# One DMA transpose in place of a plain load and TensorE transposes for the second 256 tokens of x's first two slabs, W1's second block on another queue, and a later transpose of the small vectors

## The chip, the cores and the metric

The kernel runs on one core of a Trainium2 chip. The metric is the device time of one execution, in microseconds (us); lower is better. Times of the kernel as it was come from three runs and from one execution that was taken with a hardware profiler.

## The reference

The input x has 2048 tokens of 640 features. Two results are computed from it and mixed by a gate per token.

```python
g = _sigmoid((x * gate_w).sum(-1, keepdims=True))
a = _A_ref(x, Lambda_re, Lambda_im, B_re, B_im, C_re, C_im, log_dt, Dskip)
b = _B_ref(x, w1, b1, w2, b2)
return g * a + (1 - g) * b
```

Here `_A_ref` is a state space layer: x is projected to 640 complex states (`B_bar`), a linear recurrence runs over the 2048 tokens, `h = Lam_bar * h + Bu[t]`, and the states are projected back, `2 * Re(h @ C^T) + x * Dskip`. `_B_ref` is a dense layer with 1728 hidden features, `gelu(x @ w1 + b1) @ w2 + b2`. The change concerns only how the first tokens of x and of W1 reach the first matmuls, `x @ w1`.

## The kernel before

**Tiles.** The tokens are cut into four quarters q of 512. Matmuls contract over partitions, so x is needed transposed: `xT[q]` has 128 partitions (features within a slab) by five slabs k of 128 features by 512 tokens. A "slab" of x is one k. Where x is loaded by a DMA transpose (`load_T`, L336 to L342, called by `xtrans`, L353), it lands in `xT` directly. `xn` holds x untransposed, tokens on partitions; the gates and the last stage use it.

**The first stage.** `m1_first` (L643 to L664) computes the first eight blocks of 128 hidden features (index jf) for the first quarter. All eight PSUM banks accumulate at once; the loop over slabs k is the outer one, so that work can begin when the first slab of x and the first block of W1's rows (`w1load(0, ...)`, 128 rows by 1024 columns, 256 KB) are there. For slab 0 the first six jf are done in two halves of 256 tokens each (`steps`, L648); everything else is done with 512 tokens. `w1load(k, ...)` brings W1's rows for slab k; `w1_r0` and `w1_r1` (L379) bring the other columns. After the first stage, `m1(0, NW)` (L668) goes on with the remaining jf in banks that the gelu instructions of ScalarE (L662) have freed, then `bproj(0)` projects to the states, and so on.

**How slabs 0 and 1 of x arrive.** A DMA transpose at the very start would be one way. The kernel before instead loads the first two slabs (256 features) untransposed, in two loads of 256 tokens, `xna0` and `xna1` (L369 to L371, into `xn[0]`), and TensorE transposes them against an identity (L421 to L431): `xt0` and `xt1` for the first 256 tokens of slabs 0 and 1, `xt2` and `xt3` for the second. VectorE copies each pair from PSUM to `xT` (`xc0` to `xc3`, L434). Slabs 2, 3 and 4 come by DMA transposes (L374, L376). Before that TensorE runs six matmuls on constants (`f_warm`, L413) and one more behind the first transposes (`f_fill`, L438).

**The small vectors.** Lambda, log_dt and b1 are loaded as rows of a 128 by 128 tile `rows` (L390 to L394), which GpSimd has zeroed first (`rz`, L386). One TensorE transpose, `cols` (L455), turns them into columns; VectorE copies them (L460). From there a chain of short instructions runs: exp on ScalarE (L465), angles on VectorE (L470, L485 to L493), exp and sine on ScalarE (L478, L498, L499), then the first gelu (L662). ScalarE loads an activation table ahead of exp, of sine and of gelu.

**What sets the order of work.** Nothing is ordered by hand. Every piece of work is an `op` with an engine, a modelled duration, reads and writes (from which its dependencies follow), and a priority (`Prog.op`, L157). `Sched.order` (L43 to L83) runs a list schedule on modelled times: it takes the engine that can act earliest (ties by name), and on it, among the pieces whose dependencies are done by then in the model, the one with the lowest priority number.

```python
                d_e = max(t_eng[e], min(r for _, r in released[e]))
...
            avail = [(it.prio, it.idx, it) for it, r in released[e] if r <= now + 1e-9]
            avail.sort(key=lambda x: (x[0], x[1]))
            it = avail[0][2]
```

The result is one fixed order per engine. The engines that issue DMAs here are SyncE ("sp", queue q1 in the profile), ScalarE ("act", queue q10) and GpSimd ("pool", queue q0). At the start SyncE issues, in this order: `xna0`, `xna1`, W1's second block (k=1, L372), its third block (L373), the transpose of slab 2 (L374), W1's fourth block (L375), the transpose of slabs 3 and 4 (L376), W1's fifth block (L377), the rest of W1 (L379), then the transposes of B. ScalarE issues W1's first block (L389; it reads "rz", so it is modelled to wait for GpSimd's memset, 0.2 us), then the six loads into `rows`. Matmuls get rising priorities 1, 2, 3, ... (`pe_prio`, L612); `cols` has 20.5.

**Later use of xn.** The other three slabs of the first quarter, untransposed, are loaded much later, by `xnb` (L594), for the gates.

Of the kernel before, what the change touches and what calls it, by code (L numbers as in the profile page):

```python
# [9 lines left out]
BF16 = mybir.dt.bfloat16  # L10
# [137 lines left out]
class Prog:  # L148
# [8 lines left out]
    def op(self, name, eng, dur, reads, writes, fn, prio=None, lat=0.0, after=()):  # L157
        deps = {}
        for k in reads:
            for w in self.last_w.get(k, ()):  # L160
                deps[w.idx] = w
        for k in writes:
            for w in self.last_w.get(k, ()):
                deps[w.idx] = w
            for r in self.last_r.get(k, ()):
                deps[r.idx] = r
        for a in after:
            deps[a.idx] = a
        deps = list(deps.values())
        E = self.E  # L170

        def run(eg, deps=deps, eng=eng, fn=fn):
            E.wait(eng, *[d.done for d in deps if not (eng == "pe" and d.eng == "pe")])
            return fn()

        it = self.sch.add(name, eng, dur, deps, run, prio=prio, lat=lat)
        for k in writes:
            self.last_w[k] = [it]
            self.last_r[k] = []
        for k in reads:  # L180
            self.last_r.setdefault(k, []).append(it)
        return it


def bass_gated_mix__ssm_conv_s5__dense_activation_gelu__prompt_kernel(
# [18 lines left out]
    _, S, D = A_x.shape  # L204
# [3 lines left out]
    KD = D // 128  # L208
# [13 lines left out]
    x2 = A_x[0]  # L222
# [3 lines left out]
    with ExitStack() as es:  # L226

        def SB(name, shape, dt):
            return es.enter_context(nc.sbuf_tensor(name, list(shape), dt))

        xT = [SB(f"xT_{i}", [128, KD, 512], BF16) for i in range(NQ)]
        xn = [SB(f"xn_{i}", [128, 4, D], BF16) for i in range(2)]
# [10 lines left out]
        cols = SB("cols", [128, 3 * KP + NF], FP32)  # L243
# [10 lines left out]
        ident = SB("ident", [128, 128], BF16)  # L254
# [34 lines left out]
        late = [w1f[:, i * D:(i + 1) * D] for i in range(2 * NE + 2 + NO)]  # L289
# [4 lines left out]
        PS = [es.enter_context(nc.psum_tensor(f"ps{i}", [128, 512], FP32)) for i in range(8)]  # L294
# [13 lines left out]
        op = pr.op  # L308

        def inc(eng, ins):  # L310
            return E.inc(eng, ins, eng + "_s")

        def dma_inc(eng, ins, sem):
            SEM(sem)
            E.count.setdefault(sem, 0)
            ins.then_inc(sems[sem], 16)
            E.count[sem] += 16
            return (sem, E.count[sem])

        def d_act(n):  # L320
            return 0.26 + n * 0.00084
# [4 lines left out]
        def d_mm(n):  # L326
            return n / 2400.0 + 0.004


        def load(name, eng, sem, dst, src, writes, prio, dur=0.5, lat=2.5, reads=(), after=()):  # L330
            def fn():
                with nc.allow_non_contiguous_dma(reason="columns of small vectors"):
                    return dma_inc(eng, engines[eng].dma_start(dst, src), sem)
            return op(name, eng, dur, reads, writes, fn, prio=prio, lat=lat, after=after)

        def load_T(name, sem, pairs, writes, prio, dur, lat=3.0, reads=()):  # L336
            def fn():
                t = None
                for dst, src in pairs:
                    t = dma_inc("sp", nc.sync.dma_start_transpose(dst, src), sem)  # L340
                return t
            return op(name, "sp", dur, reads, writes, fn, prio=prio, lat=lat)  # L342
# [6 lines left out]
        NW = 8  # L349
# [9 lines left out]
        def w1load(k, eng, prio, reads=()):  # L359
            edges = [0] + ([WSPLIT[k] * 128] if k in WSPLIT else []) + [FW]  # L360
            for i, (f0, f1) in enumerate(zip(edges, edges[1:])):
                load(f"w1_{k}{i}", eng, f"l_w1{k}{i}", W1sb[:, k, f0:f1], B_w1[k * 128:(k + 1) * 128, f0:f1], [("w1", k, i)], prio=prio + 0.1 * i, lat=2.6, reads=reads)

        def w1tok(k, jf):
            return ("w1", k, int(jf >= WSPLIT.get(k, NW)))

        KN = 2

        for h in range(2):  # L369
            load(f"xna{h}", "sp", f"l_xna{h}", xn[0][:, 2 * h:2 * h + 2, 0:KN * 128],  # L370
                 x2[h * 256:(h + 1) * 256, 0:KN * 128].rearrange("(c p) d -> p c d", p=128), [("xna", h)], 0.2 * h, dur=0.45, lat=2.0 + 0.4 * h)  # L371
        w1load(1, "sp", 1)  # L372
        w1load(2, "sp", 4)  # L373
        xtrans(0, range(2, 3), 5, 1.15)  # L374
        w1load(3, "sp", 6)  # L375
# [6 lines left out]
        ROWS = {"lre": (0, A_Lambda_re), "lim": (KP, A_Lambda_im), "ldt": (2 * KP, A_log_dt), "b1a": (3 * KP, B_b1[0:nmain])}  # L382
# [4 lines left out]

        op("rz", "pool", 0.2, (), list(ROWS) + [("b1b", 0), ("b1b", 1), "rz"], f_rz, prio=-90)
        w1load(0, "act", -110, reads=["rz"])  # L389
        for i, (nm, (r0, src)) in enumerate(ROWS.items()):  # L390
            src = src.rearrange("(k p) -> k p", p=128)
            load(nm, "act", "l_" + nm, rows[r0:r0 + src.shape[0], :], src, [nm], prio=-100 + i, dur=0.4)
# [25 lines left out]

        op("warm", "pe", 2.7, (), [("bank", 4)], f_warm, prio=-1000)

        for i, (k, c0, c1) in enumerate(((0, 0, 2), (1, 0, 2), (0, 2, 4), (1, 2, 4))):  # L421
            bank = (7, 6, 7, 6)[i]
            pt = PS[bank][:, :].bitcast(BF16)[:, 0:(c1 - c0) * 128]

            def f_xt(k=k, pt=pt, c0=c0, c1=c1):
                t = None
                for c in range(c0, c1):
                    t = nc.tensor.transpose(pt[:, (c - c0) * 128:(c - c0 + 1) * 128], xn[0][:, c, k * 128:(k + 1) * 128], ident[:, :])  # L428
                return inc("pe", t)

            op(f"xt{i}", "pe", 0.11 * (c1 - c0), [("xna", c0 // 2), "ident"], [("bank", bank)], f_xt, prio=-990 + i if i < 2 else 3.1 + 0.1 * i)  # L431

            def f_xc(k=k, pt=pt, c0=c0, c1=c1):
                return inc("dve", nc.vector.tensor_copy(out=xT[0][:, k, c0 * 128:c1 * 128], in_=pt))  # L434

            op(f"xc{i}", "dve", 0.42, [("bank", bank)], [("xT", 0, k, c0)], f_xc, prio=-2000 + i)

        def f_fill():  # L438
            t = None
# [1 line left out]
                t = nc.tensor.matmul(PS[3][:, 0:256], one.broadcast_to([128, 128]), one.broadcast_to([128, 256]), start=True, stop=True)  # L441
            return inc("pe", t)

        op("fill", "pe", 0.11, [("xna", 0), "ident"], [("bank", 3)], f_fill, prio=-900)

        XK0 = [[("xT", 0, k)] for k in range(KD)]
        XK0[0] = [("xT", 0, 0, 0), ("xT", 0, 0, 2)]
# [6 lines left out]
        def f_cols():  # L454
            return inc("pe", nc.tensor.transpose(psC, rows[:, :], ident[:, :]))  # L455

        op("cols", "pe", 0.3, list(ROWS) + [("b1b", 0), ("b1b", 1), "ident"], [("bank", 7)], f_cols, prio=20.5)

        def f_cols1():
            return inc("dve", nc.vector.tensor_copy(out=cols[:, :], in_=psC[:, 0:RT + 1]))  # L460
# [128 lines left out]
        for ci, src in enumerate((A_B_re, A_B_im)):  # L589
            for i, (p0, p1) in enumerate(((0, 512), (512, KP * 128))):  # L590
                load_T(f"B{ci}{i}", f"l_B{ci}{i}", [(BT[:, ci, :, p0:p1], src[p0:p1, :])], [("BT", ci, i)], prio=30 + ci + 0.1 * i, dur=0.8 * (p1 - p0) / 128)
        xtrans(1, range(KD), 32, 3.4)
        load("gwb", "sp", "l_gwb", gwb[:, :], gate_w.partition_broadcast(128), ["gwb"], prio=32.2)
        load("xnb", "sp", "l_xnb", xn[0][:, :, KN * 128:D], x2[0:512, KN * 128:D].rearrange("(c p) d -> p c d", p=128),  # L594
             [("xn", 0, 0), ("xn", 0, 1)], 32.4, dur=1.0, lat=6.0, reads=[("xna", 0), ("xna", 1)])
        big = load("w2a", "sp", "l_w2a", W2sb[:, 0:NF - 1, :], B_w2[0:nmain, :].rearrange("(j p) d -> p j d", p=128), ["w2a"], prio=33, lat=8.0)
        load("w2b", "sp", "l_w2b", W2sb[0:FL, NF - 1, :], B_w2[nmain:F, :], ["w2b"], prio=34, lat=4.0)
        load("w2c", "sp", "l_w2c", W2sb[64:64 + FL, NF - 1, :], B_w2[nmain:F, :], ["w2c"], prio=34.2, lat=4.0)
# [13 lines left out]
        def pe_prio():  # L612
            ctr["pe"] += 1
            return ctr["pe"]
# [26 lines left out]


        def m1_first():  # L643
            late = [(0, NW - 1), (1, NW - 1)]
            seq = [(k, jf) for k in range(KD) for jf in range(NW) if (k, jf) not in late]
            i = seq.index((2, NW - 1))
            seq[i:i] = late
            steps = [(0, jf, h) for h in range(2) for jf in range(6)] + [(k, jf, None) for k, jf in seq if k or jf > 5]  # L648
            for k, jf, h in steps:
                t0, t1 = (0, 512) if h is None else (256 * h, 256 * h + 256)  # L650

                def f_mm(jf=jf, k=k, t0=t0, t1=t1):
                    return inc("pe", nc.tensor.matmul(PS[jf][:, t0:t1], W1sb[:, k, jf * 128:(jf + 1) * 128], xT[0][:, k, t0:t1],  # L653
                                                      start=(k == 0 and t0 == 0), stop=(k == KD - 1), skip_group_check=jf < 6))

                op(f"m1_0_{jf}_{k}_{t0}", "pe", d_mm(t1 - t0), (XK0[k] if h is None else XK0[k][h:h + 1]) + [w1tok(k, jf)], [("bank", jf)],
                   f_mm, prio=pe_prio())
            for jf in range(NW):
                ctr["bank"] += 1

                def f_ge(jf=jf):
                    return inc("act", nc.scalar.activation(Gl[0][:, jf, :], PS[jf][:, :], ACT.Gelu_apprx_tanh, bias=b1col[:, jf:jf + 1]))  # L662

                op(f"ge_0_{jf}", "act", d_act(512), [("bank", jf), "b1col"], [("gl", 0, jf)], f_ge, prio=10)  # L664
# [344 lines left out]
        def outsT(q, mid=None):  # L1009
# [104 lines left out]
            op(f"sto{q}", "sp", 0.5, [("xn", q % 2, 0), ("xn", q % 2, 1)], [], f_st, prio=403 + q, lat=3.0)  # L1114

        m1_first()
        m1(0, NW)
        bproj(0)
# [83 lines left out]
```

## Time and profile before

| | us |
|---|---|
| median of 3 runs (lowest, highest) | 212.66 (212.58, 212.69) |
| the profiled execution's own time | 211.84 |
| its span in the trace | 210.5 |
| TensorE busy in the span | 206.9 (98%) |
| VectorE busy | 191.0 (91%) |
| ScalarE busy | 102.7 (49%) |
| DMA engines' mean share, 2 to 3 us / 5 to 6 us | 0.98 / 1.32 |

The span is the time from the first to the last instruction of the profiled execution; about 1.3 us lie around it. Starts in the timeline are us from the span's start. "PE" is TensorE's matmuls, "PEld" its weight loads, "DVE" VectorE, "ACT" ScalarE, "SPq" and "ACTq" the instructions by which SyncE and ScalarE issue DMAs. A line such as L653 is a line of the kernel. Matmuls are pipelined and their ends are modelled: a busy TensorE may still be short of its peak, and the distance from one start to the next says more than a duration. Where many DMAs overlap, the DMA share can come out above 1.

### The profile page before, as it was taken

What the parts mean: (1) busy time and instruction counts of PE and PEld (TensorE: products, weight loads), DVE (VectorE), ACT (ScalarE), POOL (GpSimd) and SP (SyncE); (2) the same over time, 40 slices, a digit from 0 to 9 for tenths busy, and PEclk for the clock granted to TensorE, in tenths of its full rate; (3) what the DMA queues carried; (4) which work ended last, traced back from release to release, by engine and by line L of the source; (5) the groups of instructions that cost most, each with busy time, mean ns of one, the idle gap of its engine ahead of it and who ended that gap; (6) DMA issues with size and microseconds to landing.
All of it is one profiled execution on the core that took longest, in us unless ns stands there. A gap on an engine that the chain in (4) does not pass through costs nothing.

```text
span 210.5 us, 2557 instructions
## 1 busy us (share of the span) xinstructions
PE 206.9 (98%) x987; PEld 95.1 (45%) x1004; DVE 191.0 (91%) x244; ACT 102.7 (49%) x166; POOL 4.2 (2%) x12
## 2 busy tenths in 40 slices
PE   8999999999999999999999999999999999999996
PEld 4544444444444444444444444444444444444444
DVE  2499999999999999999999999899999999899482
ACT  2398556679850533556683222455664253204321
POOL 1000000030000000000000000000010000000000
DMA  6999999999500020053373000006631000006623
GB/s 191 271 230 124 200 204 226 361 190 207 129 0 4 0 50 0 0 107 65 80 61 113 3 0 0 0 2 140 142 87 58 0 0 4 0 2 145 135 71 100
DMA packets 50248, 19.47 MB, mean 93 GB/s; under 512 B 43068, under 2 KB 48828, under 8 KB 50236
## 3 DMA queue, kind: packets, MB, share of 16 engines
q1 hardware_dynamic: 47904, 17.59, 38.2%
q0 software_dynamic: 1600, 1.32, 4.3%
q10 hardware_dynamic: 732, 0.40, 0.7%
q8 instruction: 8, 0.13, 0.3%
q14 instruction: 4, 0.03, 0.1%
HBM read 8.68 MB, written 2.63 MB: 54 GB/s over the span
## 4 chain that ended last, share of the span: by engine, by line
PE 98%; issue 0%; DVE 0%
PE ps L675 22%; PE ps L718 20%; PE ps L1015 20%; PE ps L1085 15%; PE ps L809 5%; PE ps L653 4%; PE ps L922 4%; PE ps L829 1%; PE ps L416 1%; PE ps L696 1%; PE ps L882 1%; PE ps L1050 1%; PE ps L428 0%; PE ps L846 0%; DVE W1sb L954 0%
## 5 line engine op out<-in xcount | busy, mean ns | idle before, releaser
L675 PE MATMUL ps<-xT,W1sb 128*128 128x512 bf16 x214 | 47.5, 379 | 0.3
L762 DVE TENSOR_TENSOR_SCAN W<-atab,V 128x1280 bf16<-128x1280 f32 x16 | 44.3, 2812 | 0.3
L718 PE MATMUL ps<-xT,BT 128*128 128x512 bf16 x196 | 43.3, 379 | 0.2
L1015 PE MATMUL ps<-Gl,W2sb 128*128 128x512 bf16 x192 | 42.8, 379 | 0.2
L682 ACT ACTIVATE Gl<-ps,cols 128x512 bf16<-128x512 f32 x44 | 29.8, 695 | 15.5 <-PE ps L675 15.5
L675 PEld LDWEIGHTS ps<-xT,W1sb 128*128 128x128 bf16 x220 | 21.5, 98 | 26.0
L1085 PE MATMUL ps<-Hb,CT 128*128 128x512 bf16 x150 | 32.9, 379 | 0.0
L729 ACT ACTIVATE U<-ps 128x512 bf16<-128x512 f32 x40 | 23.7, 596 | 15.5 <-PE ps L718 15.5
L718 PEld LDWEIGHTS ps<-xT,BT 128*128 128x128 bf16 x200 | 19.4, 98 | 23.8 <-ACT Gt L704 0.4
L1015 PEld LDWEIGHTS ps<-Gl,W2sb 128*128 128x128 bf16 x195 | 18.9, 98 | 23.3 <-issue 0.7
L1023 ACT ACTIVATE E1T<-ps,cols 128x512 bf16<-128x512 f32 x15 | 10.0, 686 | 26.2 <-PE ps L1015 14.7
L1085 PEld LDWEIGHTS ps<-Hb,CT 128*128 128x128 bf16 x150 | 14.7, 98 | 17.7
L1093 ACT ACTIVATE E2T<-ps 128x512 bf16<-128x512 f32 x15 | 9.0, 597 | 21.7 <-PE ps L1085 21.7
L627 DVE SCALAR_TENSOR_TENSOR trf<-xn,gwb 128x640 bf16<-128x640 bf16 x16 | 13.2, 823 | 0.4
L505 DVE TENSOR_TENSOR V<-V,W 128x1280 bf16<-128x1280 bf16 x16 | 12.5, 821 | 0.3
L505 DVE TENSOR_TENSOR Hb<-Hb,V 128x1280 bf16<-128x1280 bf16 x16 | 12.5, 821 | 0.3
L505 DVE TENSOR_TENSOR V<-mr,U 128x2560 bf16<-128x2560 bf16 x8 | 11.9, 1492 | 0.3
L505 DVE TENSOR_TENSOR Hb<-c,W 128x2560 bf16<-128x2560 bf16 x8 | 11.9, 1490 | 0.2
L809 PE MATMUL ps<-W2sb,Gl 128*128 128x512 bf16 x51 | 11.8, 379 | 0.1
L505 DVE TENSOR_TENSOR V<-s,W 128x2560 bf16<-128x2560 bf16 x8 | 11.9, 1484 | 0.0
L505 DVE TENSOR_TENSOR W<-mi,U 128x2560 bf16<-128x2560 bf16 x8 | 11.9, 1483 | 0.0
L1073 ACT ACTIVATE xT<-xT,cols 128x512 bf16<-128x512 bf16 x15 | 10.0, 712 | 0.0
(103 smaller groups left out, 148.2 us busy)
## 6 DMA issues: line engine op xcount, KB each, us to landing
W2sb<-in_B_w_dram SPq DMA_DIRECT2D x1, 2080.0 KB, 8.4
out_dram<-xn SPq DMA_DIRECT2D x3, 640.0 KB, 5.5
xn<-in_A_x_dram POOLq DMA_DIRECT2D x2, 640.0 KB, 7.0
W1sb<-in_B_w_dram SPq DMA_DIRECT2D x4, 256.0 KB, 4.0
trf<-grow SPq DMA_DIRECT2D x4, 256.0 KB, 4.9
xn<-in_A_x_dram SPq DMA_DIRECT2D x1, 640.0 KB, 7.2
W1sb<-in_B_w_dram SPq DMA_DIRECT2D x1, 480.0 KB, 5.6
W1sb<-in_B_w_dram SPq DMA_DIRECT2D x1, 400.0 KB, 6.4
```

Of the source, the lines that this page charges most:

```text
L505: return inc("dve", nc.vector.tensor_tensor(out=o, in0=a, in1=b, op=o_))
L627: t = inc("dve", nc.vector.scalar_tensor_tensor(out=scr[:, :], in0=xn[q % 2][:, c, :], scalar=1.0, in1=gwb[:, :], op0=ALU.mult, op1=ALU.mu ...
L675: t = nc.tensor.matmul(PS[bank][:, :], W1sb[:, k, jf * 128:(jf + 1) * 128], xT[q][:, k, :], start=(k == 0), stop=(k == KD - 1))
L682: return inc("act", nc.scalar.activation(Gl[q % 2][:, jf, :], PS[bank][:, :], ACT.Gelu_apprx_tanh, bias=b1col[:, jf:jf + 1]))
L718: t = nc.tensor.matmul(PS[bank][:, :], BT[:, ci, kd, k * 128:(k + 1) * 128], xT[q][:, kd, :], start=(kd == 0), stop=(kd == KD - 1))
L729: return inc("act", nc.scalar.activation(dst, src, ACT.Copy, scale=1.0 if ci == 0 else -1.0))
L762: t = inc("dve", nc.vector.tensor_tensor_scan(out=g[:, ci, :], data0=a, data1=v[:, ci, :], initial=0.0, op0=ALU.mult, op1=ALU.add))
L809: t = nc.tensor.matmul(PS[bank][:, :], Gl[q % 2][:, jf, t4 * 128:(t4 + 1) * 128], W2sb[:, jf, 0:DN], start=False, stop=False, skip_group_c ...
L1015: t = nc.tensor.matmul(PS[bank][:, :], W2sb[:, jf, d * 128:(d + 1) * 128], Gl[q % 2][:, jf, :], start=(jf == 0 and not lead), stop=(jf == ...
L1023: return inc("act", nc.scalar.activation(E1T[:, d, :], PS[bank][:, :], ACT.Identity, bias=cols2[:, 0, d:d + 1]))
L1073: return inc("act", nc.scalar.activation(xT[q][:, d, :], xT[q][:, d, :], ACT.Copy, scale=cols2[:, 1, d:d + 1]))
L1085: t = nc.tensor.matmul(PS[bank][:, :].rearrange("p (s t) -> p s t", s=2), CT[:, ci, k, d * 128:(d + 1) * 128], Hb[:, 2 * (q % 2):2 * (q % ...
```

## The change

The second 256 tokens of slabs 0 and 1 no longer come by `xna1`, four TensorE transposes and two VectorE copies. One DMA transpose on SyncE's queue, `xTa`, writes them into `xT[0]`. The first 256 tokens come as before (the load is now called `xna`). W1's second block moves from SyncE's queue to ScalarE's, with priority -109 and no reads. `cols` moves from priority 20.5 to 23.5. In `m1_first`, seven jf instead of six are done in halves for slab 0. Later, `xnb` becomes two loads, one of three slabs for the first 256 tokens and one of all five slabs for the second 256 tokens.

```diff
--- before.py
+++ after.py
@@ -366,10 +366,8 @@
 
         KN = 2
 
-        for h in range(2):
-            load(f"xna{h}", "sp", f"l_xna{h}", xn[0][:, 2 * h:2 * h + 2, 0:KN * 128],
-                 x2[h * 256:(h + 1) * 256, 0:KN * 128].rearrange("(c p) d -> p c d", p=128), [("xna", h)], 0.2 * h, dur=0.45, lat=2.0 + 0.4 * h)
-        w1load(1, "sp", 1)
+        load("xna", "sp", "l_xna", xn[0][:, 0:2, 0:KN * 128], x2[0:256, 0:KN * 128].rearrange("(c p) d -> p c d", p=128), ["xna"], 0, dur=0.45, lat=2.0)
+        load_T("xTa", "l_xTa", [(xT[0][:, 0:KN, 256:512], x2[256:512, 0:KN * 128])], [("xT", 0, k, 2) for k in range(KN)], 0.2, 1.2, lat=2.0)
         w1load(2, "sp", 4)
         xtrans(0, range(2, 3), 5, 1.15)
         w1load(3, "sp", 6)
@@ -387,6 +385,7 @@
 
         op("rz", "pool", 0.2, (), list(ROWS) + [("b1b", 0), ("b1b", 1), "rz"], f_rz, prio=-90)
         w1load(0, "act", -110, reads=["rz"])
+        w1load(1, "act", -109)
         for i, (nm, (r0, src)) in enumerate(ROWS.items()):
             src = src.rearrange("(k p) -> k p", p=128)
             load(nm, "act", "l_" + nm, rows[r0:r0 + src.shape[0], :], src, [nm], prio=-100 + i, dur=0.4)
@@ -418,22 +417,22 @@
 
         op("warm", "pe", 2.7, (), [("bank", 4)], f_warm, prio=-1000)
 
-        for i, (k, c0, c1) in enumerate(((0, 0, 2), (1, 0, 2), (0, 2, 4), (1, 2, 4))):
-            bank = (7, 6, 7, 6)[i]
-            pt = PS[bank][:, :].bitcast(BF16)[:, 0:(c1 - c0) * 128]
-
-            def f_xt(k=k, pt=pt, c0=c0, c1=c1):
+        for k in range(KN):
+            bank = 7 - k
+            pt = PS[bank][:, :].bitcast(BF16)[:, 0:256]
+
+            def f_xt(k=k, pt=pt):
                 t = None
-                for c in range(c0, c1):
-                    t = nc.tensor.transpose(pt[:, (c - c0) * 128:(c - c0 + 1) * 128], xn[0][:, c, k * 128:(k + 1) * 128], ident[:, :])
+                for c in range(2):
+                    t = nc.tensor.transpose(pt[:, c * 128:(c + 1) * 128], xn[0][:, c, k * 128:(k + 1) * 128], ident[:, :])
                 return inc("pe", t)
 
-            op(f"xt{i}", "pe", 0.11 * (c1 - c0), [("xna", c0 // 2), "ident"], [("bank", bank)], f_xt, prio=-990 + i if i < 2 else 3.1 + 0.1 * i)
-
-            def f_xc(k=k, pt=pt, c0=c0, c1=c1):
-                return inc("dve", nc.vector.tensor_copy(out=xT[0][:, k, c0 * 128:c1 * 128], in_=pt))
-
-            op(f"xc{i}", "dve", 0.42, [("bank", bank)], [("xT", 0, k, c0)], f_xc, prio=-2000 + i)
+            op(f"xt{k}", "pe", 0.22, ["xna", "ident"], [("bank", bank)], f_xt, prio=-990 + k)
+
+            def f_xc(k=k, pt=pt):
+                return inc("dve", nc.vector.tensor_copy(out=xT[0][:, k, 0:256], in_=pt))
+
+            op(f"xc{k}", "dve", 0.42, [("bank", bank)], [("xT", 0, k, 0)], f_xc, prio=-2000 + k)
 
         def f_fill():
             t = None
@@ -441,7 +440,7 @@
                 t = nc.tensor.matmul(PS[3][:, 0:256], one.broadcast_to([128, 128]), one.broadcast_to([128, 256]), start=True, stop=True)
             return inc("pe", t)
 
-        op("fill", "pe", 0.11, [("xna", 0), "ident"], [("bank", 3)], f_fill, prio=-900)
+        op("fill", "pe", 0.11, ["xna", "ident"], [("bank", 3)], f_fill, prio=-900)
 
         XK0 = [[("xT", 0, k)] for k in range(KD)]
         XK0[0] = [("xT", 0, 0, 0), ("xT", 0, 0, 2)]
@@ -454,7 +453,7 @@
         def f_cols():
             return inc("pe", nc.tensor.transpose(psC, rows[:, :], ident[:, :]))
 
-        op("cols", "pe", 0.3, list(ROWS) + [("b1b", 0), ("b1b", 1), "ident"], [("bank", 7)], f_cols, prio=20.5)
+        op("cols", "pe", 0.3, list(ROWS) + [("b1b", 0), ("b1b", 1), "ident"], [("bank", 7)], f_cols, prio=23.5)
 
         def f_cols1():
             return inc("dve", nc.vector.tensor_copy(out=cols[:, :], in_=psC[:, 0:RT + 1]))
@@ -591,8 +590,10 @@
                 load_T(f"B{ci}{i}", f"l_B{ci}{i}", [(BT[:, ci, :, p0:p1], src[p0:p1, :])], [("BT", ci, i)], prio=30 + ci + 0.1 * i, dur=0.8 * (p1 - p0) / 128)
         xtrans(1, range(KD), 32, 3.4)
         load("gwb", "sp", "l_gwb", gwb[:, :], gate_w.partition_broadcast(128), ["gwb"], prio=32.2)
-        load("xnb", "sp", "l_xnb", xn[0][:, :, KN * 128:D], x2[0:512, KN * 128:D].rearrange("(c p) d -> p c d", p=128),
-             [("xn", 0, 0), ("xn", 0, 1)], 32.4, dur=1.0, lat=6.0, reads=[("xna", 0), ("xna", 1)])
+        for h in range(2):
+            f0 = KN * 128 * (1 - h)
+            load(f"xnb{h}", "sp", f"l_xnb{h}", xn[0][:, 2 * h:2 * h + 2, f0:D], x2[h * 256:(h + 1) * 256, f0:D].rearrange("(c p) d -> p c d", p=128),
+                 [("xn", 0, h)], 32.4 + 0.1 * h, dur=0.6, lat=6.0, reads=["xna"])
         big = load("w2a", "sp", "l_w2a", W2sb[:, 0:NF - 1, :], B_w2[0:nmain, :].rearrange("(j p) d -> p j d", p=128), ["w2a"], prio=33, lat=8.0)
         load("w2b", "sp", "l_w2b", W2sb[0:FL, NF - 1, :], B_w2[nmain:F, :], ["w2b"], prio=34, lat=4.0)
         load("w2c", "sp", "l_w2c", W2sb[64:64 + FL, NF - 1, :], B_w2[nmain:F, :], ["w2c"], prio=34.2, lat=4.0)
@@ -641,17 +642,16 @@
 
 
         def m1_first():
-            late = [(0, NW - 1), (1, NW - 1)]
-            seq = [(k, jf) for k in range(KD) for jf in range(NW) if (k, jf) not in late]
+            seq = [(k, jf) for k in range(1, KD) for jf in range(NW) if (k, jf) != (1, NW - 1)]
             i = seq.index((2, NW - 1))
-            seq[i:i] = late
-            steps = [(0, jf, h) for h in range(2) for jf in range(6)] + [(k, jf, None) for k, jf in seq if k or jf > 5]
+            seq[i:i] = [(0, NW - 1), (1, NW - 1)]
+            steps = [(0, jf, h) for h in range(2) for jf in range(NW - 1)] + [(k, jf, None) for k, jf in seq]
             for k, jf, h in steps:
                 t0, t1 = (0, 512) if h is None else (256 * h, 256 * h + 256)
 
                 def f_mm(jf=jf, k=k, t0=t0, t1=t1):
                     return inc("pe", nc.tensor.matmul(PS[jf][:, t0:t1], W1sb[:, k, jf * 128:(jf + 1) * 128], xT[0][:, k, t0:t1],
-                                                      start=(k == 0 and t0 == 0), stop=(k == KD - 1), skip_group_check=jf < 6))
+                                                      start=(k == 0 and t0 == 0), stop=(k == KD - 1), skip_group_check=jf < NW - 1))
 
                 op(f"m1_0_{jf}_{k}_{t0}", "pe", d_mm(t1 - t0), (XK0[k] if h is None else XK0[k][h:h + 1]) + [w1tok(k, jf)], [("bank", jf)],
                    f_mm, prio=pe_prio())
```

## The prediction

> **What bounds the kernel now.** I read the page first: busy shares and the chain that ended last.
>
> ```profile
> PE 206.9 (98%) x987; PEld 95.1 (45%) x1004; DVE 191.0 (91%) x244; ACT 102.7 (49%) x166; POOL 4.2 (2%) x12
> ...
> PE 98%; issue 0%; DVE 0%
> ```
>
> TensorE carries the end: nothing but matmuls stands in the chain. So a change counts only as far as it removes matmul time, or moves the moment from which TensorE never waits again. To find that moment I read the timeline of the first 14 us (start, duration, what, and in brackets the idle time before it).
>
> ```profile
> 0.74 0.97 SPq L333 DMA_DIRECT2D xn<-in_A_x_dram  x2
> ...
> 0.97 0.40 ACTq L333 DMA_DIRECT2D W1sb<-in_B_w_dram  x1
> ...
> 2.74 1.20 SPq L340 DMA_TRANSPOSE xT<-in_A_x_dram  x1
> 3.06 0.49 PEld L428 LDWEIGHTS ps<-ident,xn 128*128 128x128 bf16 x4 [0.47 <-DMA xn<-in_A_x_dram]
> ...
> 3.98 0.34 PEld L653 LDWEIGHTS ps<-xT,W1sb 128*128 128x128 bf16 x3 [0.33 <-DVE xT L434]
> ...
> 4.55 0.39 PE L428 MATMUL ps<-ident,xn 128*128 128x128 bf16 x4
> ...
> 5.21 2.06 PEld L653 LDWEIGHTS ps<-xT,W1sb 128*128 128x128 bf16 x14 [0.23 <-DVE xT L434]
> ...
> 7.60 0.22 PE L455 MATMUL ps<-ident,rows 128*128 128x128 bf16 x1
> ...
> 12.06 2.42 ACT L662 ACTIVATE Gl<-ps,cols 128x512 bf16<-128x512 f32 x4
> ```
>
> Three waits: for x (to 3.06), for the first copy (to 3.98), for the copy of the second 256 tokens (to 5.21). After 5.21 the matmuls run back to back into the second stage: each 512-column matmul starts 0.216 us after the last, each 256-column one 0.109. The first matmul with W1's second block (k=1) starts at 6.09. I call that moment K; everything behind it follows at a fixed distance, so the change is worth what it does to K, plus any new wait behind it.
>
> Then I asked for the DMA issues in narrow windows (KB, us from issue to landing). The first four rows are the first x load, W1's first block, the first DMA transpose of x, and a transpose of the same size at 204 us, when the DMA engines are nearly idle; the last two are the queues between 2.65 and 3.0 us (packets, MB, share).
>
> ```profile
> xn<-in_A_x_dram SPq DMA_DIRECT2D x1, 128.0 KB, 2.3
> ...
> W1sb<-in_B_w_dram ACTq DMA_DIRECT2D x1, 256.0 KB, 2.8
> ...
> xT<-in_A_x_dram SPq DMA_TRANSPOSE x1, 4.2
> ...
> Gl<-xT SPq DMA_TRANSPOSE x1, 2.4
> ```
>
> ```profile
> q10 hardware_dynamic: 63, 0.13, 96.2%
> q1 hardware_dynamic: 1, 0.00, 0.2%
> ```
>
> The x load lands at 3.04, W1's first block at 0.97+2.8 = 3.77, the second x load at 1.27+2.9 = 4.17. In that window ScalarE's queue (q10) has the engines to itself, though SyncE had issued the second x load from 1.27 to 1.71. The packet records agree: transfers of both queues are served in order of issue. W1's first block has its packets at 2.33 to 3.31, the second x load from 3.05, and ScalarE's tiny row loads, issued at 1.40, 2.01, 2.31 and 2.65, are served at 3.35, 3.88, 4.20 and 4.46, with SyncE's W1 blocks (issued 1.75 and 2.27) in between. The engines are busy from 2 us on (share 0.93 or more in each us to 11), so a transfer put ahead of another delays it by its full length.
>
> **The change, part by part.**
>
> Removed from TensorE: the four transposes at 4.55, which took 0.22 us (4.55 to 4.77), and the wait of about 0.11 for the second copy (the matmul before started at 4.99, the next could have at 5.10). Twelve 256-column matmuls and one 512 become fourteen 256s: 14 x 0.109 against 12 x 0.109 + 0.216, 0.00. The two removed VectorE copies free nothing that is late. If the data were in time, fourteen halves from 3.99 (three at the slow pace seen until 4.49: 0.185 and 0.213 apart) would put the second seven at 4.99 and K at 4.99+0.76 = 5.75, 0.34 earlier.
>
> Are they in time? The moved load of W1's second block has no reads, while the first block still reads the zeroed rows. The program's scheduler takes, at time 0, the lowest priority among what is *released*: on ScalarE only the second block is, the first comes free at 0.2. So I expect ScalarE to issue the **second block first**, at about 0.74 (its first DMA is at 0.97 today because of that wait), and the first block at about 1.2. Each block is 8 packets of 2 KB on each of 16 engines, at 84 ns: 0.67 us. By order of issue the first block's last data moves from 3.40 to 4.07 and its landing from 3.77 to 4.44. The first half then starts at 4.48 instead of 3.99, and the second seven can start at 4.48+0.76 = 5.24.
>
> The new transpose is issued at 1.27 and takes SyncE 1.2 us, as the row at 2.74. Its landing is not in the trace. Bounds: 2.4 us after issue (the idle row) is 3.7; 4.3 us (the second transpose of x today, behind other loads) is 5.57. By the queue: after the first block's data at 4.07, 0.75 for its 512 packets (the idle transpose: 205.47 to 206.22) and 0.47 to landing gives 5.29. I take that, since the engines are full as at 2.74. The second seven start at 5.33 and K is 6.10.
>
> The first x load and W1's second block are now issued at the same moment. If x goes second, it lands 0.67 later, at 3.71, the first half starts 0.95 behind that (today 3.04 to 3.99), at 4.66, and K is 6.19. I take the middle, 6.15: 0.06 later than today.
>
> [...]
>
> SyncE's queue: x load 0.48, transpose 1.2, W1's third block 0.48 put the next transpose at about 2.95 instead of 2.74. What is behind it waits for engines anyway; per engine, 32 packets of 18 ns replace 16 of 27, 0.14 us more, so later landings move by 0.15 to 0.25. W1's third block and its x slice land at 6.4 and 6.95 and are needed at K+1.51 = 7.66; the next at 7.9 and 8.9, needed near 9.8; W1's rest at 12.25, needed at 13.27. All have cover of 0.5 or more. ScalarE's row loads come 0.2 later: the last lands near 7.0, needed at 7.9. The second slab load of x later is 128 KB larger and split in two (one more SyncE issue, about 0.45), behind 24 us, where the next matmuls' operands land 4 us early: 0.
>
> The cols transpose now stands two matmuls further back (behind the second of k=2 instead of the last of k=1), 0.43 later against K. Behind it hangs a strict chain: VectorE copy, exp, angles, sine, table load, first gelu at 12.06, done at 12.75. The first matmul of the next stage (weights loaded at 13.05, matmul 13.27) needs that gelu's bank. At +0.43 the gelu ends at 13.18, weights at 13.22, the matmul at 13.32: 0.05 of wait, between 0 and 0.1. VectorE starts its tables as much later; its first result that TensorE needs is ready at 67.9 and used at 71.8, so that costs nothing.
>
> Sum: +0.06 + 0.05 = +0.11. The profiled execution took 211.84 us (span 210.5); the median of the runs is 212.66. I add the difference to the median: 212.77, say 212.8. This kernel's measurement tells about 0.2% (0.43 us) from no change.
>
> **Rivals.**
>
> *A, the blocks come in time* (first block first, or both served together): K 5.75, less 0.34, plus 0.05: 212.4, at best 212.2 when the gelu wait is absent and the first half comes earlier. For it: the issue order is my reading of the scheduler. Against: with two blocks on one queue the engines are full anyway.
>
> *B, the queues take turns*, slower. If after the second block the engines turn to SyncE's transpose before ScalarE's first block, that block lands another 0.58 to 0.75 later, at 5.02 to 5.19. Fourteen halves of 0.109 start 0.04 behind: K 6.59 to 6.76, +0.50 to 0.67, plus 0.05: 213.2 to 213.4. It decides when the first block lands after 4.9 us. For it: a few row packets at 3.47 to 3.56 slipped between packets of the second x load. Against: the order of the other rows above. [...]
>
> *C, the transpose itself is late*: slower by over 0.43 once the second seven start after 5.70 (5.70+0.77-6.09+0.05). At 5.57 plus the 0.2 by which x and W1 crowd it, K is 6.58: 213.2. Against: the idle row's 2.4.
>
> *D, the slow pace lasts*: TensorE now idles from about 3.8 to 4.5, and the doubling of pace at 4.49 may come only after as long a run again (0.78 to 4.49, 3.7 us). Half of 3.7 is lost: +1.85, 214.6. Against: today it came in spite of 0.17 us of idling. [...]
>
> **How the numbers follow.** Forecast 0.53 (0.02 of it above +0.43), A 0.14 (0.05 of it below -0.43, if I have mis-sized it), B 0.14, C 0.10, D 0.09. Faster 0.05; slower 0.02+0.14+0.10+0.09 = 0.35; the same 0.60. The range 212.3 to 213.4 takes in A's main part, the forecast, B and most of C, and leaves out D, A's edge and the tails, about 0.19. The forecast's own range is 212.6 to 213.0.
>
> **What would show it.** ScalarE's first W1 issue at about 0.74 without a wait, the second at 1.2; the first 256-column matmul near 4.5 instead of 3.99, waiting for a DMA; seven and seven halves at 0.109; K near 6.15; a bank wait of at most 0.1 near 13.3. A first half at 3.99 shows the issue order wrong; a first half at 5.1 shows B; a wait between the sevens of over 0.4 shows C; 0.213 spacing after 4.6 shows D.

## The result and the profile after

The changed kernel takes 214.48 us (median of 4 runs, 214.04 to 214.95) against 212.62 us beside it: a ratio of 1.0092 (95% interval 1.0066 to 1.0118), slower by 1.86 us. In a later batch the ratio was 1.0085 (1.0067 to 1.0103). The forecast was 212.8 us with a range to 213.4.

The profiled execution took 214.35 us, its span 213.0 us, 2.5 more than the profiled one before (which, at 211.84, lies below the median of its kernel). Busy shares and chain, from the page of the changed kernel:

```profile
PE 209.4 (98%) x1001; PEld 95.6 (45%) x1001; DVE 190.4 (89%) x242; ACT 102.7 (48%) x166; POOL 4.2 (2%) x12
...
PE 97%; DMA 2%; DVE 0%; issue 0%
```

TensorE still carries the end, but the load of x now stands at the head of the chain, with 2% of the span. By the page, TensorE's busy time *rose* by 2.5 us although four transposes left it. Some 0.9 us of that is not real: the kernel before has 987 matmul records for 1004 weight loads, and each of the 17 that are missing leaves an empty 0.05 us in its trace. The other 1.6 us are, and busy time that grows with less work means that the same matmuls took longer. The timeline of the changed kernel's first 9 us:

```profile
0.74 0.46 SPq L333 DMA_DIRECT2D xn<-in_A_x_dram  x1
0.75 0.91 ACTq L333 DMA_DIRECT2D W1sb<-in_B_w_dram  x2
...
1.26 1.27 SPq L340 DMA_TRANSPOSE xT<-in_A_x_dram  x1
...
4.35 0.34 PEld L427 LDWEIGHTS ps<-ident,xn 128*128 128x128 bf16 x4 [1.76 <-DMA xn<-in_A_x_dram]
...
5.14 3.12 PEld L653 LDWEIGHTS ps<-xT,W1sb 128*128 128x128 bf16 x16 [0.34 <-DVE xT L433]
5.17 4.19 PE L653 MATMUL ps<-xT,W1sb 128*128 128x256 bf16 x17
```

ScalarE issues its first W1 block at 0.75, without the wait that put it at 0.97 before: that is the second block, as the scheduler's rule says. x lands at 4.31 instead of 3.02, the first transposes start at 4.36 instead of 3.19, the first half at 5.17 instead of 3.99. The wait of 1.76 us for x is that of the weight loads; the matmuls on constants last until 3.19, so TensorE itself idles for 1.17 us of it. Now the pace. The next line is the stretch of the fourteen halves in the changed kernel (stretch, its length, TensorE busy and matmuls that fall in it, granted clock, DMA share, GB/s):

```profile
5.17:8.11 2.94, 2.94 (x15) 1.00 1.18 228
```

Fourteen matmuls of 256 columns took 2.94 us, 0.21 each, where the kernel before took 0.109 each from 4.55 on. The granted clock reads 1.00 all the same, so only the distance between starts shows the slow pace. It lasts until 8.96 us: two matmuls of 512 columns still take 0.427 each, then the distance falls to 0.216.

That accounts for the whole 2.5 us of the two profiled spans: the first half 1.18 later; from there to K 2.94 instead of 2.10 (+0.84: fourteen halves at 0.109 take 1.53, so the pace costs 1.41, and the transposes' 0.22, the wait of 0.11 and some 0.24 of slow pace that the old order had are gone); two slow 512-column matmuls +0.42; and 0.05 of bank wait before the next stage (15.51 to 15.78 is 0.27, where 0.216 is the rule). Sum +2.49. From there on both kernels run alike.

### The profile page after: what moved, and what is told of

It is laid out like the page before. It is cut to its first block, busy times and chain, and to the rows that moved or that the text cites. A ratio compares the mean times of both kernels' runs of the same rounds, so it can differ in the third digit from the quotient of the medians.

```text
span 213.0 us, 2567 instructions
## 1 busy us (share of the span) xinstructions
PE 209.4 (98%) x1001; PEld 95.6 (45%) x1001; DVE 190.4 (89%) x242; ACT 102.7 (48%) x166; POOL 4.2 (2%) x12
## 3 DMA queue, kind: packets, MB, share of 16 engines
HBM read 8.68 MB, written 2.63 MB: 53 GB/s over the span
## 4 chain that ended last, share of the span: by engine, by line
PE 97%; DMA 2%; DVE 0%; issue 0%
PE ps L675 22%; PE ps L718 20%; PE ps L1015 20%; PE ps L1085 15%; PE ps L809 5%; PE ps L653 5%; PE ps L922 4%; DMA xn<-in_A_x_dram 2%; PE ps L829 1%; PE ps L696 1%; PE ps L882 1%; PE ps L1050 1%; PE ps L427 0%; PE ps L846 0%; DVE W1sb L954 0%; PE ps L844 0%
## 5 line engine op out<-in xcount | busy, mean ns | idle before, releaser
L675 PE MATMUL ps<-xT,W1sb 128*128 128x512 bf16 x220 | 48.1, 379 | 0.0
L718 PE MATMUL ps<-xT,BT 128*128 128x512 bf16 x200 | 43.8, 379 | 0.0
L653 PE MATMUL ps<-xT,W1sb 128*128 128x512 bf16 (+1 forms) x47 | 10.7, 400 | 0.0
```

The costliest lines, as they stand in the source:

```text
L675: t = nc.tensor.matmul(PS[bank][:, :], W1sb[:, k, jf * 128:(jf + 1) * 128], xT[q][:, k, :], start=(k == 0), stop=(k == KD - 1))
L718: t = nc.tensor.matmul(PS[bank][:, :], BT[:, ci, kd, k * 128:(k + 1) * 128], xT[q][:, kd, :], start=(kd == 0), stop=(kd == KD - 1))
```

## The experiments

**Theory T**: ScalarE issues W1's second block first, beside the load of x and ahead of the first block; so x and the first block are late, TensorE idles, and because of the idling its slow pace lasts some microseconds more. **Rival R**: the new DMA transpose, or two W1 blocks on ScalarE's queue in whatever order, crowds the start. All ratios are to the kernel before on the same chip, with 95% intervals.

**First block first.** The second block is made to wait for the zeroed rows too, so that the priorities decide.

```diff
-        w1load(1, "act", -109)
+        w1load(1, "act", -109, reads=["rz"])
```

> The changed kernel, but the load of W1's second block also reads the zeroed rows, so that ScalarE issues the first block before the second; nothing else moves. Theory T (the cost is the issue order at the start: the second block runs beside the x load and ahead of the first block, TensorE idles from 3.2 to 4.4 us, and its slow pace then lasts for some 4 us more): ScalarE's first issue is back at about 0.97 us and is the first block, x lands near 3.1, the first half starts at 4.0 to 4.1, the pace doubles near 4.5, K (first matmul of k=1) is 5.8 to 6.2, time 212.3 to 212.8. Rival R (the DMA transpose at the start, or two W1 blocks on ScalarE's queue at all, crowds x and the first block): x still lands at 3.8 or later, K above 7.5, time 213.8 or more.

Measured: 212.52 us, ratio 1.0025 (1.0013 to 1.0038): most of the loss is gone, 0.5 us is left. x lands at 3.40, the first block at 4.00, the first half starts at 4.18, at the fast pace already. What is left stands in the timeline of TensorE's weight loads:

```profile
4.18 0.66 PEld L653 LDWEIGHTS ps<-xT,W1sb 128*128 128x128 bf16 x7 [0.39 <-DVE xT L433]
5.90 1.09 PEld L653 LDWEIGHTS ps<-xT,W1sb 128*128 128x128 bf16 x10 [1.05 <-DMA xT<-in_A_x_dram]
```

After seven halves the weight loads wait 1.05 us for the DMA transpose, which lands at 5.85; the matmuls lose 0.94 by it. K is 6.67: outside what T gave (5.8 to 6.2), short of what R gave (above 7.5). So the issue order is the main cause, and with it mended the transpose is the next to be late: case C of the prediction. To that extent R holds: with both W1 blocks on ScalarE's queue the transpose landed at 5.4 to 5.9 in all five profiles, with the second on SyncE's at 4.8 to 4.9 in three.

**The queue move alone.** The kernel before, with only the second block moved.

```diff
-        w1load(1, "sp", 1)
...
         w1load(0, "act", -110, reads=["rz"])
+        w1load(1, "act", -109)
```

> The kernel before, with only W1's second block moved to ScalarE's queue without reads (no DMA transpose for x, cols in its old place; the scheduler puts one pair of the second transposes ahead of the first halves). Theory T: nearly the whole loss is here: x lands at 4.0 to 4.4 us, first half at 5.0 to 5.4 at the slow pace, K near 8, time 214.0 to 215.0. Rival R in its form that the DMA transpose does the harm: 212.4 to 213.0.

Measured: 214.37 us, ratio 1.0115 (1.0099 to 1.0130). The move of one load, without the DMA transpose, loses as much as the whole change. x lands at 3.91, the first half starts at 5.22, the slow pace lasts to 7.3, K is 7.66. Part of the delay is this kernel's own: its order puts a pair of the second transposes ahead of the first half, and they wait for the second x load, which lands at 4.99, while W1's first block was there at 4.72.

**The transpose alone.** The changed kernel with the second block back on SyncE's queue.

```diff
+        w1load(1, "sp", 1)
         w1load(2, "sp", 4)
...
-        w1load(1, "act", -109)
```

> The changed kernel with W1's second block back on SyncE's queue, behind the new DMA transpose: the transpose for the second 256 tokens, the seven halves and the two late x loads stay. Theory T: x lands at 3.0 and the first block at 3.8 as before the change, first half at 4.0, the transpose lands at 4.7 to 5.3, K 5.75 to 6.2, W1's second block (issued near 2.5) lands near 5.9 and may hold K by 0.1; time 212.2 to 212.7. Rival R: the transpose delays x or the first block, or lands after 5.7 itself, K above 6.6, time 213.1 or more.

Measured: 212.03 us, ratio 0.9992 (0.9978 to 1.0006): no difference. The weight loads of its start:

```profile
4.02 1.97 PEld L653 LDWEIGHTS ps<-xT,W1sb 128*128 128x128 bf16 x14 [0.33 <-DVE xT L433]
6.17 0.76 PEld L653 LDWEIGHTS ps<-xT,W1sb 128*128 128x128 bf16 x5 [0.17 <-DMA W1sb<-in_B_w_dram]
```

Fourteen halves without a break: the transpose lands at 4.92, 3.6 us after its issue, in time. But they are not all fast. The slow stretch and the fast one read

```profile
4.02:5.24 1.22, 1.22 (x8) 1.00 0.73 215
5.24:6.11 0.87, 0.87 (x10) 1.00 0.94 323
```

The slow pace lasted to 5.2 us here, against 4.5 in the profile before, and the fourteen halves took 2.09 us. Then W1's second block, issued only at 2.59 behind the transpose's 1.2 us of issue, lands at 6.12 and holds K until 6.17. It cost the matmuls only 0.06 us in this execution, but it would have held K there had the halves been fast. R falls here in its form that the transpose at the start, by itself, does harm.

**A longer warm-up.** The changed kernel, with its matmuls on constants stretched over the time in which it waits for x.

```diff
-            for n in (512,) * 5 + (384,):
+            for n in (512,) * 8 + (192,):
```

> The changed kernel with the matmuls on constants at the start longer by 1344 columns (to about 4.3 us instead of 3.2), so that TensorE does not idle until x lands; the DMAs are untouched. If the slow pace lasted because of the idling (T): the pace doubles by 4.5 to 5.2, fourteen halves from about 5.2 at 0.109 give K near 6.7 and 213.2 to 213.5, and the runs scatter less than the 0.9 us of the changed kernel. If the late data alone are the cost, or the pace does not depend on the gap: K stays near 8.1 and the time at 214.2 to 214.8.

Measured: 212.48 us, ratio 1.0020 (1.0007 to 1.0032), and its ten runs lie within 0.4 us (212.36 to 212.74). Not one DMA was changed: x still lands late, at 3.87 (its transposes start at 4.30, when the longer warm-up ends), and the first half still starts at 5.11. But the stretch of the fourteen halves reads

```profile
5.11:6.80 1.69, 1.69 (x15) 1.00 1.00 242
```

1.69 us instead of 2.94. The ratio falls from 1.0085 (the changed kernel in the other batch, see below) to 1.0020, and the time lies below even what T gave. So of some 1.8 us, about 1.4 are the slow pace (0.0065 of 212.2 us) and 0.4 are left for the late data; the two ratios come from two batches.

**A shorter warm-up before the change.** The same question from the other side: the kernel before, all DMAs as they were, but TensorE idle from 2.0 us until x lands.

```diff
-            for n in (512,) * 5 + (384,):
+            for n in (512,) * 3:
```

> The kernel before with its matmuls on constants cut from 2944 columns to 1536, so that TensorE idles from about 2.1 us until x lands at 3.0, some 1.0 us, as long as in the changed kernel (1.2); every DMA and every other instruction stays. If idling alone keeps the slow pace (T): the first half still starts at 4.0, but the halves and the first 512-column matmuls run at 0.213 and 0.427 until 7 to 9 us, and the time is 213.0 to 214.2 against 212.2 to 212.6 of the kernel before. If the pace depends on the time since the first matmul only: the pace doubles near 4.5 and the time does not change.

Measured: 213.02 us, ratio 1.0044 (1.0030 to 1.0058), from idling alone. The profiled execution was the shortest of its eleven runs (212.37), and even there the pace stays slow to 6.0 us (4.5 in the profile before; T gave 7 to 9): the first line is the slow stretch, in which eight halves and the four second transposes take 2.09 us; the second the fast one, four halves in 0.46.

```profile
3.87:5.96 2.09, 2.09 (x13) 1.00 1.34 282
5.96:6.42 0.46, 0.46 (x5) 1.00 0.69 77
```

**Two other orders of the loads.** First, W1's second block on ScalarE's queue behind two row loads:

```diff
-        w1load(1, "act", -109)
+        w1load(1, "act", -98.5, reads=["rz"])
```

> The changed kernel with W1's second block on ScalarE's queue behind two of the row loads (issue near 2.3 us), so that x, W1's first block and the new transpose go ahead of it. T: x lands at 3.0 to 3.4, first half near 4.1, the transpose at 4.8 to 5.3, the second block at 5.6 to 6.1, K 5.8 to 6.2, time against before -0.3 to +0.2 us. If the transpose needs 4.5 us from its issue whatever runs beside it: it lands at 5.7 to 5.9, K near 6.6, +0.4 to +0.6 us.

Measured: 213.34 us, ratio 1.0063 (1.0038 to 1.0087): a miss. The transpose landed as the second case gave, but K is 6.96 and the loss of some 1.3 us is more than either case had. x lands at 3.03, but the first block, though issued at 0.98 as before the change, lands only at 4.70, the transpose at 5.80 and the second block at 6.91, each of them waited for:

```profile
4.80 0.67 PEld L653 LDWEIGHTS ps<-xT,W1sb 128*128 128x128 bf16 x7 [1.15 <-DVE xT L433]
5.84 0.66 PEld L653 LDWEIGHTS ps<-xT,W1sb 128*128 128x128 bf16 x7 [0.36 <-DMA xT<-in_A_x_dram]
6.95 0.33 PEld L653 LDWEIGHTS ps<-xT,W1sb 128*128 128x128 bf16 x3 [0.45 <-DMA W1sb<-in_B_w_dram]
```

(The first wait is put down to the copy of x, long done; it was for W1's first block, which landed at 4.70.) Between 3.8 and 4.2 us the engines moved only 84 GB/s. Why the first block took 3.7 us here and 3.0 with the second block right behind it stays open.

Second, x first on ScalarE's queue and the transpose first on SyncE's:

```diff
-        load("xna", "sp", "l_xna", ..., 0, dur=0.45, lat=2.0)
+        load("xna", "act", "l_xna", ..., -120, dur=0.45, lat=2.0)
...
+        w1load(1, "sp", 1)
...
-        w1load(1, "act", -109)
```

> The changed kernel with the x load first on ScalarE's queue, then W1's first block; the new transpose is the first issue of SyncE, then W1's second block. If the transpose's landing is set by its issue and by what is ahead of it: it lands at 4.0 to 4.7, x at 3.0 to 3.6, the first block at 3.9 to 4.4, the second block at 5.4 to 5.9; K 5.8 to 6.2 and -0.3 to +0.2 us against before. If the transpose, now served beside x, delays it: x lands at 3.8 or later, TensorE idles 0.7 us or more, and the slow pace lasts: +0.8 us or more.

Measured: 212.60 us, ratio 1.0026 (1.0008 to 1.0045). x lands at 3.09, the transpose at 4.76, but the first block at 4.55, so TensorE idles 0.87 us before the first half (4.69) and the slow pace lasts to 6.6. A miss too: x was not delayed, yet both W1 blocks (the second at 6.47) and K (7.13) are later than the first case gave. These two profiles have the same matmuls up to 3.82 us, and then a gap of 1.0 us (first order) and 0.9 us (second). Behind it the pace was fast at once in the first (the weight loads of seven halves took 0.67 us) and slow for two more us in the second: a gap of that size did not bring the slow pace in both.

**The changed kernel again**, beside these on one chip.

> The changed kernel once more, beside the others on one chip: +1.5 to +2.2 us against before; x lands at 3.9 to 4.4 us, first half near 5.1, and the moment at which the pace doubles is not fixed but lies anywhere from 6 to 9 us, which is the scatter of its runs.

Measured: 213.75 us, ratio 1.0085 (1.0067 to 1.0103). The kernel before has its median at 212.19 in the first batch and 212.15 in this one, so ratios are compared across the two. The profiled execution is the shortest of its runs (213.41): first half at 5.08, pace fast from 7.3, K at 7.64. In the first profile of the same kernel it was fast from 8.96 and the time was 214.35. Where the slow pace ends differs from run to run, and the time with it.

**Smaller gaps.** The transpose alone, and the kernel before, each with 64 more columns of warm-up and one more 128-column matmul on constants behind the first transposes.

```diff
-            for n in (512,) * 5 + (384,):
+            for n in (512,) * 5 + (448,):
...
-            for _ in range(1):
+            for n in (256, 128):
```

> The run with the DMA transpose alone (W1's second block on SyncE's queue), with 64 more columns in the matmuls on constants at the start and one more 128-column matmul on constants behind the first transposes, so that TensorE's two short idle times (some 0.05 us before x, 0.15 us before the first half) close. If even such gaps put off the end of the slow pace: the pace doubles before 4.7 us, the first seven halves take less than 1.2 us instead of 1.4, and the time is 0.2 to 0.6 us below the kernel before (a version that beats both). If gaps of this size do not matter: -0.3 to +0.1 us, as without the additions.

> The kernel before with the same two additions and nothing else. If gaps of 0.15 us matter: 0.1 to 0.4 us below the kernel before and less scatter; if not: within 0.1 us of it.

Measured: 212.04 us, ratio 0.9998 (0.9988 to 1.0009), and 212.12 us, ratio 1.0004 (0.9991 to 1.0016). Neither differs from the kernel before, and no version beat it. Whether such small gaps matter to the pace is not settled by this. In the profile of the first, W1's first block landed at 4.12, so a gap of 0.26 us was left before the first half, and the pace stayed slow to 6.6 us (the first line, eleven halves). In the profile of the second the pace doubled at 4.0, but its weight loads then waited for W1's second block, which landed at 6.19 (the second line), so that K is 6.23.

```profile
4.25:6.55 2.30, 2.30 (x11) 1.00 0.94 263
...
6.23 0.76 PEld L653 LDWEIGHTS ps<-xT,W1sb 128*128 128x128 bf16 x5 [0.53 <-DMA W1sb<-in_B_w_dram]
```

## Why the prediction was wrong

**Right: the issue order.** ScalarE issues the second block first, at 0.75 and the first at 1.22 (forecast: 0.74 and 1.2). **Right: the bank wait** from the later cols transpose, 0.05 as forecast. **Right: everything behind K** is covered; no load of the first stage other than those named was waited for.

**Wrong: that the two queues' transfers are served in order of issue.** I had read that from one window of the trace before. In the changed kernel the second block and x are issued at the same moment. The block's packets start at 1.81 and have the engines alone until 2.47, and x then shares them to the end. In the window from 2.9 to 3.4 us (queue, packets, MB, share) it reads:

```profile
q10 hardware_dynamic: 68, 0.12, 63.0%
q1 hardware_dynamic: 138, 0.07, 45.2%
```

So x is late twice over. Its first packet comes 0.63 us later than before (2.47 against 1.84), which is the forecast's worse branch. Its 128 KB are then drawn out between the 512 KB of both W1 blocks: from first packet to last they take 1.46 us instead of 0.79, which the forecast did not have. x lands at 4.31, where the worse branch had 3.71; the first block lands at 5.04, where it had 4.44. The trace before could have told: between 2.35 and 2.6 us, when the first x load (q1) and W1's first block (q10) both have packets, it reads

```profile
q10 hardware_dynamic: 17, 0.03, 62.6%
q1 hardware_dynamic: 91, 0.04, 61.0%
```

The window on which the forecast rested, 2.65 to 3.0, lies between the two x loads: the first has its last packet at 2.63 and the second its first at 3.05, 1.8 us after its issue. Why it starts so late no run shows. The interleaving that I had kept for case B, and given 0.14, stands in both windows: 68 packets of ScalarE's queue and 138 of SyncE's in the one, 17 and 91 in the other. This mis-sized term put the first half at 5.17 instead of 4.48 to 4.66. With the warm-up stretched, about 0.4 us is left for the late data (interval 0.15 to 0.68), near case B's 0.55 to 0.72.

**Wrong: that the slow pace ends at 4.5 whatever TensorE does.** The forecast ran all fourteen halves at 0.109, so its sum had nothing for a slow pace; in the changed kernel they ran at 0.213, and two more matmuls at 0.427. This was the larger error, some 1.4 us: case D, with a chance of 0.09, was priced at +1.85 and 214.6, and the measured time is 214.48. That the numbers meet is in part luck. D's price was all pace; the measured loss is some 1.4 of pace and 0.4 of late data. The step that failed is leaving this term out of the sum: I had seen that TensorE would idle 0.7 us and took its going fast in spite of 0.17 us of idling for evidence against. It idled 1.17 us (3.19 to 4.36), because x was later than forecast.

The runs show that idling alone costs this: with no DMA changed, a gap of 0.9 us costs 0.9 us in the kernel before, and filling the gap gives some 1.4 us back in the changed one. They do not show what exactly ends the slow pace. In the six profiles without a gap over 0.3 us ahead of it, it ended at 3.6, 4.0, 4.5, 5.2, 5.5 and 6.6 us; with gaps of 0.8 us and more it ended at 6.0, 6.6, 7.3, 7.3 and 9.0, and once before 4.8 (the row-load order, where the gap came after 3.8). So the two groups touch: with such a gap the end came at 6.0 us or later in five profiles of six, without one at 5.5 or earlier in five of six. In these profiles a gap neither set the end nor was needed for a late one.

**Half right: the transpose.** It landed at 5.79 in the changed kernel (forecast 5.29), which cost nothing there, because the slow halves needed it only at 6.62. Where the halves were fast (first block first) it cost 0.94 us. Two terms were too small: its last packet went at 5.04 (forecast 4.82), and it landed 0.75 behind that (0.47 in the idle row). In the eight profiles that have this transpose the second term lies between 0.6 and 1.4.

**Where the expected gain went.** Four transposes and a wait of 0.11 did leave TensorE. With the transpose alone the halves run unbroken, and two things take the 0.34 us that the forecast saw in it back. In the first profile the slow pace made the halves 0.33 us longer than the forecast's 1.76, and W1's second block, pushed back by the transpose's 1.2 us of issue, would have held K at 6.17 in any case. In the profile with smaller gaps that block landed at 5.55, and the slow pace and a late first half alone put K at 6.89. The engines are busy from 2 us on (a share of 0.93 or more in each us to 11 in the profile before), and where a load was put earlier another came later: in the first of these profiles W1's second block landed at 6.12 instead of the 5.57 before the change, in the second W1's first block at 4.12 instead of 3.77.

## What to carry to other kernels

At the start of a kernel, look at what a load is put *ahead of*: a scheduler that picks by priority among released work lets the load without a dependency go first, and here, with a block of 256 KB beside the first load of 128 KB, the first half started at 5.17 us instead of 3.99. Count the idle time of TensorE before its first real matmuls twice, once as waiting and once as a slow pace behind it (here 1.17 us of idling, and slow halves from 5.17 on that cost 1.41 us), and try matmuls on constants in it if the data cannot come sooner (here the fourteen halves then took 1.69 us instead of 2.94). Read the pace from the distance between starts (0.213 us against 0.109), since here neither the busy share (98%) nor the granted clock (1.00) showed it.

## What the runs showed of the hardware

In these profiles TensorE at half pace counts as busy with a granted clock of 1.00: fourteen matmuls of 256 columns took 2.94 us in one kernel and 1.69 in another. The end of the slow pace moved between 3.6 and 9.0 us in twelve profiles; in the two of the changed kernel it was 7.3 and 9.0, with times of 213.41 and 214.35 us. The DMA transpose of the second 256 tokens (128 KB) landed 3.6 to 4.6 us after its issue beside other loads; one of the same size in the kernel before, with the engines nearly idle, landed 2.4 us after its issue.
